# Rows of the main expert slots turned by DMA in 16-bit planes, in place of transposes on TensorE

## The chip, the cores and the metric

The kernel runs on one core of one Trainium2 chip. Its time is the device time of one execution in microseconds (us). Three executions of the kernel before took 737.18 to 739.1 us, with a median of 738.54 us. A fourth execution, taken with the hardware profiler, took 740.14 us; all rows below come from it.

## The reference

The kernel computes feature-map attention and sends the result through a mixture of eight experts, everything in float32. Cut to what matters:

```
q_p, k_p = phi(q), phi(k)                 # exp(+-(x @ w_phi - max|x @ w_phi|))
x  = (q_p @ (k_p^T v)) / (q_p . sum k_p)  # 8 x 8 heads, 576 tokens of 64 -> 4608 tokens of 512
logits = x @ w_gate;  local = sigmoid(x @ w_local)
e  = argmax(logits) if first token or local < 0.5 else the expert of the token before
out = softmax(logits)[e] * (relu(x @ w1[e]) @ w2[e])   # w1[e]: 512 x 1024, w2[e]: 1024 x 512
```

## The kernel before

**Two halves.** The first half (to about 290 us) is the attention and the gate. It writes the 4608 rows of x (512 floats each) to DRAM as `xs`. The second half is the mixture of experts, and only its later part is touched by the change.

**Slots.** Tokens are sorted by expert into units of 128 rows. A slot is one expert with the units that it works on: a quad has 4 units, a trip 3, a pair 2. A dual is one unit of two half-filled experts, and reads both experts' weights. Two early trips run while the gate is being finished. Then the method `moe` runs the eleven main slots, one after another: quad Q0, trip T0, dual D0, Q1, T1, Q2, D1, T2, Q3, T3 and the pair P.

**A slot's work.** `layer1` multiplies the slot's transposed rows with eight column blocks of w1 and `layer2` multiplies the result unit by unit with w2. Every float32 product is made of three products of two-part numbers (`three`, lines 1114 to 1116: high by high, low by high, high by low). So each operand is needed as a high part (rounded by ScalarE) and a low part (the rest, subtracted by VectorE). A quad's layer 1 is 8 x 12 matmuls of 512 columns, a trip's 8 x 12 of 384 columns; layer 2 is 24 matmuls of 512 columns for each unit. The results `y` of a unit are scaled by VectorE (line 1216) and scattered to DRAM by an indirect DMA on GpSimd's queue (`out`, line 1219).

**Weights.** Each slot reads eight blocks of 512 KB on SyncE's queue (line 980) into raw buffers `wraw` (five of them). ScalarE rounds a block (`whi`, line 991) and VectorE subtracts (`wlo`, line 994) into one of thirteen pairs of buffers. Blocks are loaded ahead, as soon as buffers come free. A dual's blocks go straight into the pairs, sixteen DMAs of 512 KB.

**The rows of the next slot.** They are fetched by an indirect DMA on GpSimd's queue (`gather_x`, line 1038) as token by feature tiles `xg`, 128 x 512, of which there are six buffers. TensorE must have them as feature by token. `tokens` does this: it hands `layer2` of the slot in front a list of steps, and after the first three matmuls of layer 2 a step transposes up to four units in TensorE, eight transposes of 64 rows a unit (`rows`, line 1096), into PSUM tiles `tr`. `parts` then makes the high part on ScalarE (line 1109, or 1107 for a dual) and the low part on VectorE (line 1110). Where the next slot is a dual, the dual's unit and those of the slot behind it are prepared together, during the slot in front of the dual. So 28 of the main slots' 32 units are transposed in this way, in eight places: 3 in Q0, 4 + 1 in T0, 3 in Q1, 4 in T1, 4 in Q2, 4 in T2, 3 in Q3 and 2 in T3. Q0's own four units are transposed earlier, by another method.

**Order.** A scheduler places the instructions of each engine; the method `past` holds an instruction behind a marked one on its own engine. Each engine works its instructions off in order, and DMAs issued by one engine stand in that engine's queue.

Of the kernel before, what the change touches and what calls it, by code (L numbers as in the profile page):

```python
# [7 lines left out]
F32 = mybir.dt.float32  # L8
F32R = mybir.dt.float32r
BF16 = mybir.dt.bfloat16  # L10
I32 = mybir.dt.int32
AF = mybir.ActivationFunctionType
ALU = mybir.AluOpType
AX = mybir.AxisListType
# [4 lines left out]
DM, E, FF = 512, 8, 1024  # L19
# [37 lines left out]
class Kernel:  # L57
# [9 lines left out]
    def run(self):  # L67
        nc, tc, A = self.nc, self.tc, self.A
        act, dve = self.act, self.dve
        with ExitStack() as root:  # L70
# [13 lines left out]
            warm = self.const.tile([128, E], BF16, name="warm")  # L84
            act.activation(warm, self.cnt, AF.Exp)

# [182 lines left out]
    def proj(self, p):  # L269
# [18 lines left out]
        for sg in (0, 1):  # L288
            self.last_act = act.activation(kp[:, :, :, sg, :].rearrange("p c h f -> p h c f"), sb[:, :, :, 0], AF.Exp,  # L289
                                           scale=1.0 - 2 * sg)  # L290
# [17 lines left out]
    def qexp(self, p, pj):  # L308
# [3 lines left out]
        for sg in (0, 1):  # L312
            self.act.activation(qp[:, sg].rearrange("p h (c r k) -> p (h c) r k", c=2, r=2), src, AF.Exp,  # L313
                                scale=1.0 - 2 * sg)
# [265 lines left out]
    def gate(self, bp):  # L580
        tc, pe, act, dve, pool, ident = self.tc, self.pe, self.act, self.dve, self.pool, self.ident

        def sm(shape, name, dt=F32):
            return self.small.tile(shape, dt, name="g_" + name)
# [51 lines left out]
        yield  # L636
        ci = sm([9, 128], "ci", I32)
        dve.tensor_scalar_max(ci, sc, cm)
# [32 lines left out]
        yield  # L671
        ri = self.back2.tile([128, NC], I32, name="ri")
        dve.tensor_copy(ri, rf)
# [3 lines left out]
        ex = sm([128, NC, E], "ex")  # L677
        act.activation(ex, ls, AF.Exp)
        yield
# [61 lines left out]
    def experts(self, es, name):  # L741
        ei = self.psm([NU, 1], "ei" + name, I32)
        self.dve.tensor_scalar_min(ei, es, float(E - 1))
        return ei

    def fetch(self, es, k, n, name, wait, halves=()):
# [3 lines left out]
        dve.scalar_tensor_tensor(row, es, float(NU_E), k, ALU.mult, ALU.add)  # L750
        ri = self.psm([NU, 1], "ri" + name, I32)

# [26 lines left out]
        t = self.pst([128, 2, n])  # L779
        tok = self.psm([128, n], "tok" + name, I32)  # L780
        prob = self.psm([128, n], "prob" + name)
# [7 lines left out]
    def units_so_far(self, add, shift, name):  # L789
# [4 lines left out]
        t = self.moved(t, [NU, E], "u" + name)  # L794
        u = self.psm([NU, E], "u" + name, I32)
        with self.soon():
# [272 lines left out]
    def tokens(self, slots, late=False):  # L1069

        for s in slots:
            if "xg" not in s:
                self.gather_x(s)
        units, g = [(s, k) for s in slots for k in range(s["n"])], 1 if late else 4

        def step(group):
            if late:
                self.whole(*group[0], group[0][1] % 3 == 2, self.here())
                return
            out = []  # L1080
            for n, (s, k) in enumerate(group):
                if n % 2 == 0:
                    t = self.halfbanks()
                c = slice(n % 2 * 256, n % 2 * 256 + 256)
                out.append((s, k, t[:, :, c]))
                self.rows(out[-1][2], s["xg"][k])
            for s, k, t in out:
                self.unrow(s, *self.into(s), k * 128, t)
        return [lambda a=a: step(units[a:a + g]) for a in range(0, len(units), g)]

    def rows(self, t, src):

        for d in range(4):
            for r in (0, 1):
                k = slice(64 * r, 64 * r + 64)
                self.pe.transpose(t[:, r, d * 64:d * 64 + 64], src[k, d * 128:d * 128 + 128], self.ident[k, k])  # L1096
# [40 lines left out]
    def layer1(self, s, between):  # L1137
# [9 lines left out]
        for f0 in range(0, 8, per):  # L1147
# [10 lines left out]
            hc = slice(f0, f0 + per)  # L1158
            self.marks[act] = act.activation(hh[:, hc, :], t, AF.Relu)  # L1159
            self.marks[dve] = dve.scalar_tensor_tensor(hl[:, hc, :], t, 0.0, hh[:, hc, :].bitcast(F32),  # L1160
# [5 lines left out]
    def layer1_one(self, s, between):  # L1166
# [7 lines left out]
        def turn(q):  # L1174
            t = self.halfbanks()[:, :, 0:256]
            self.rows(t, hs[:, q * 512:q * 512 + 512])
            hc = slice(q * 4, q * 4 + 4)
            self.unrow(s, hh[:, hc], hl[:, hc], 0, t)
        for q in range(4):
            t = self.psl.tile([128, 256], F32, name="l1")  # L1180
            for d in range(4):
                self.both(s, q, t, xh[:, d, x], xl[:, d, x], slice(d * 256, d * 256 + 256), d == 0, d == 3)
                if d == 0 and q == 3:
                    turn(0)
            self.marks[act] = act.activation(hs[:, q * 256:(q + 1) * 256], t, AF.Relu)
            if between:
# [5 lines left out]
    def layer2(self, s, between, held=None):  # L1192
        tc, dve, pool = self.tc, self.dve, self.pool
        hh, hl = s["h"]
        self.need(s, 8) if len(s["ei"]) == 1 else None
        for k in range(s["n"]):
            if hasattr(self, "psr"):
                t = self.psr.tile([128, DM], F32, name="l2")
            else:
                t = self.psb.tile([128, DM], F32, name="l2", tag="nm")  # L1200
            o = slice(k * 128, k * 128 + 128)
            for f in range(8):
                c = slice((f % 2) * DM, (f % 2) * DM + DM)
                self.both(s, 4 + f // 2, t, hh[:, f, o], hl[:, f, o], c, f == 0, f == 7)
                if f in ((0, 2) if s["n"] > 1 else (1, 3, 5)) and between:
                    between.pop(0)()
                if f % 2 and k == s["n"] - 1:
                    self.used(1)
                elif f % 2:
                    self.spare()  # L1210
            y = self.mx2.tile([128, DM], F32, name="y", bufs=3)
            u = s["u"] + k
            if s in self.eslots:
                self.marks[self.act] = self.act.mul(y, t, s["prob"][:, u:u + 1])
            else:
                self.marks[dve] = dve.tensor_scalar_mul(y, t, s["prob"][:, u:u + 1])  # L1216

            def put(y=y, at=s["tok"][:, u:u + 1]):
                ins = pool.indirect_dma_start(self.A["out"], bass.IndirectOffsetOnAxis(at, 0), y, None,  # L1219
                                              bounds_check=NT - 1, oob_is_err=False)  # L1220
                tc.declare_no_dep(ins.ins, group="outs", reason="each token is written once")
                tc.add_to_no_dep_group("outs", ins.ins)
            if held is None:
                put()
            else:
                held.append(put)

    def slots(self, order, held=None, soon=(), later=()):
        first = order[0]
        if "x" not in first:  # L1230
            if first is self.eslots[0]:
                self.first_tokens(first)
            else:
                for f in self.tokens([first]):
                    f()
        self.held = first.get("asked", len(first.get("w", ())))
        self.coming, self.loaded = list(order), getattr(self, "loaded", [])
        self.marks = {self.sp: self.marks[self.sp]} if soon or held is not None else {}
        for i, s in enumerate(order):
            while s.get("asked", len(s.get("w", ()))) < 8:  # L1240
                self.spare()
            self.need(s, 4)
            new = order[i + 1] if i + 1 < len(order) else None
            ahead = order[i + 1:i + 3 if new and len(new["ei"]) == 2 and s["n"] > 1 else i + 2]
            between = self.tokens([x for x in ahead if "x" not in x], bool(soon) and i == 0)
            if s["n"] > 1:
                self.layer1(s, list(soon[i]) if i < len(soon) else [])
                rest = between
            else:
                rest = self.layer1_one(s, between) + between  # L1250
            if i < len(later):
                rest = list(later[i]) + rest
            self.layer2(s, rest, None if new else held)
            for f in rest:
                f()
            s.clear()
# [131 lines left out]
```

## Time and profile before

| what | value |
|---|---|
| median of three executions | 738.54 us (737.18 to 739.1) |
| profiled execution | 740.14 us, of which the span is 738.4 us |
| granted TensorE clock over the span | 0.998 of full speed |
| TensorE matmul busy | 718.3 us (97%) |
| VectorE, ScalarE, GpSimd busy | 446.8, 348.9, 183.2 us |
| DMA, mean over the span | 169 GB/s |

The span runs from the first to the last instruction of the program; 1.7 us lie around it. A main slot shows in the timeline of TensorE as a run of `l<-xhi,..` matmuls (layer 1) and a run of `l<-whi,hh` matmuls (layer 2). The main slots take the span from 363 us to its end.

### The profile page before, as it was taken

To read this page: it belongs to the slowest core of one execution; us is meant where nothing else is said; L and a number is where in the kernel's file an instruction comes from. 1 tells how busy PE (TensorE), PEld (TensorE's weight loads), DVE (VectorE), ACT (ScalarE), POOL (GpSimd) and SP (SyncE) were. 2 spreads that over 40 slices of the span, in tenths; PEclk is the share of its full clock that TensorE was granted. 3 is DMA by queue.
4 is the path that set the end of the run, shared out by engine and by line. 5 is a ranking of instruction groups with operands and counts; after the bars stand their busy time and mean duration, and the time that the engine had idled before them with its cause. 6 is when DMAs were issued, how large, how long until landed. Compare 5 with 4: busy or idle time off the path is not lost.

```text
span 738.4 us, 22173 instructions
## 1 busy us (share of the span) xinstructions
PE 718.3 (97%) x9447; PEld 630.2 (85%) x9447; DVE 446.8 (61%) x814; ACT 348.9 (47%) x673; POOL 183.2 (25%) x305
## 2 busy tenths in 40 slices
PE   7999999999989999999999999999999999999996
PEld 6999999999979988888888975889888778888995
DVE  5898898889978885583436335445523365444413
ACT  4777776777667763333534125333312245241301
POOL 0211002420265674363403041021302102101011
PEclk9999999999999999999999999999999999999999
DMA  7765544555476842064819966335676365434100
GB/s 208 230 188 143 159 133 136 152 150 143 131 250 189 250 136 66 10 214 133 317 65 335 327 235 221 122 129 172 226 296 242 120 220 171 143 128 158 58 40 30
DMA packets 66101, 125.05 MB, mean 169 GB/s; under 512 B 7220, under 2 KB 45300, under 8 KB 65950
## 3 DMA queue, kind: packets, MB, share of 16 engines
q1 hardware_dynamic: 57808, 101.03, 43.1%
q0 software_dynamic: 8016, 22.51, 8.6%
q8 instruction: 75, 1.23, 0.7%
q14 instruction: 26, 0.21, 0.1%
q10 hardware_dynamic: 176, 0.07, 0.0%
HBM read 102.05 MB, written 22.06 MB: 168 GB/s over the span
## 4 chain that ended last, share of the span: by engine, by line
PE 52%; issue 0%; DVE 0%; POOLq 0%; another core or an unknown queue 0%; POOL 0%
PE l L1114 16%; PE l L1115 15%; PE l L1116 15%; PE l L1127 4%; PE tr L1096 1%; PE tr L1066 0%; DVE wlo L994 0%; POOLq L1384 0%; DVE y L1216 0%; POOLq L1302 0%; POOLq L1303 0%; POOL out L1219 0%; POOLq L1219 0%
## 5 line engine op out<-in xcount | busy, mean ns | idle before, releaser
L1159 ACT ACTIVATE hh<-l 128x384 fp32r<-128x384 f32 (+1 forms) x84 | 45.1, 537 | 197.4 <-PE l L1116 161.2
L1114 PE MATMUL l<-xhi,whi 128*128 128x384 f32 (+2 forms) x352 | 123.8, 352 | 0.0
L1116 PE MATMUL l<-xhi,wlo 128*128 128x384 f32 (+2 forms) x352 | 123.2, 350 | 0.0
L1115 PE MATMUL l<-xlo,whi 128*128 128x384 f32 (+2 forms) x352 | 123.1, 350 | 0.0
L1160 DVE SCALAR_TENSOR_TENSOR hl<-l,hh 128x384 fp32r<-128x384 f32 (+1 forms) x84 | 51.6, 614 | 116.6 <-ACT hh L1159 113.5
L994 DVE TENSOR_TENSOR wlo<-wraw,whi 128x1024 fp32r<-128x1024 f32 x80 | 96.6, 1223 | 32.3 <-ACT whi L991 32.0
L1114 PE MATMUL l<-whi,hh 128*128 128x512 f32 x288 | 114.1, 396 | 0.0
L1115 PE MATMUL l<-wlo,hh 128*128 128x512 f32 x288 | 112.4, 390 | 0.3 <-DVE wlo L994 0.3
L1116 PE MATMUL l<-whi,hl 128*128 128x512 f32 x288 | 112.4, 390 | 0.0
L289 ACT ACTIVATE kp<-sb 128x512 f32<-128x512 f32 x144 | 83.4, 624 | 59.4 <-DVE sb L285 51.9
L283 DVE TENSOR_REDUCE m<-pj 128x8 f32<-128x1024 f32 x72 | 87.9, 1221 | 26.9 <-PE pj L280 22.1
L991 ACT CAST whi<-wraw 128x1024 fp32r<-128x1024 f32 x80 | 82.1, 1047 | 29.3 <-PE l L1116 14.9
L285 DVE TENSOR_TENSOR sb<-pj,m 128x1024 f32<-128x1024 f32 x72 | 88.2, 1225 | 4.4
L408 PE MATMUL nm<-kvs,qp 128*64 128x74 f32 x2304 | 88.7, 228 | 2.1 <-issue 1.5
L280 PE MATMUL pj<-first,kq 64*128 64x128 f32 x1152 | 85.8, 290 | 4.6 <-DMA kq<-in_kqT 4.2
L313 ACT ACTIVATE qp<-pj 128x512 f32<-128x512 f32 x144 | 79.9, 597 | 13.4 <-PE pj L298 12.5
L1219 POOL DMA_INDIRECT out<-y,p_tokm x32 | 36.9, 1154 | 198.8 <-DVE y L1216 179.2
L408 PEld LDWEIGHTS nm<-kvs,qp 128*64 128x64 f32 x2304 | 80.7, 136 | 3.2 <-issue 2.1
L280 PEld LDWEIGHTS pj<-first,kq 64*128 64x128 f32 x1152 | 72.0, 192 | 10.6 <-issue 4.1
L330 PE MATMUL kvp<-v,kp 128*64 128x65 f32 x2048 | 77.3, 226 | 1.5 <-issue 1.3
L1114 PEld LDWEIGHTS l<-xhi,whi 128*128 128x128 f32 x352 | 66.2, 188 | 7.0 <-issue 1.6
L330 PEld LDWEIGHTS kvp<-v,kp 128*64 128x64 f32 x2048 | 67.5, 139 | 4.7 <-issue 1.5
(226 smaller groups left out, 916.5 us busy)
## 6 DMA issues: line engine op xcount, KB each, us to landing
wraw<-in_w1h SPq DMA_DIRECT2D x44, 512.0 KB
wraw<-in_w2h SPq DMA_DIRECT2D x44, 512.0 KB
kq<-in_kqT SPq DMA_DIRECT2D x47, 384.0 KB
v<-in_va SPq DMA_DIRECT2D x48, 195.0 KB
xs<-xo SPq DMA_DIRECT2D x48, 128.0 KB
whi<-in_w1h SPq DMA_DIRECT2D x8, 512.0 KB
wlo<-in_w1h SPq DMA_DIRECT2D x8, 512.0 KB
whi<-in_w2h SPq DMA_DIRECT2D x8, 512.0 KB
```

Source lines behind the costliest of these rows:

```text
L280: self.last_pe = self.pe.matmul(t[:, h, i % 2, j, :], kq[r, j, s], self.w2[r], start=True, stop=True)
L283: dve.tensor_reduce(m, f, AX.X, ALU.max, apply_absolute_value=True)
L285: self.last_dve = dve.tensor_sub(sb.rearrange("p h c j f -> p (h c j) f"), f, m.unsqueeze(2).broadcast_to([128, 8, 128]))
L289: self.last_act = act.activation(kp[:, :, :, sg, :].rearrange("p c h f -> p h c f"), sb[:, :, :, 0], AF.Exp, scale=1.0 - 2 * sg)
L313: self.act.activation(qp[:, sg].rearrange("p h (c r k) -> p (h c) r k", c=2, r=2), src, AF.Exp, scale=1.0 - 2 * sg)
L330: self.pe.matmul(t[r, sg, h], kp[:, h, sg, r], v[:, h], start=first and sg + h == 0, stop=last and sg + h == 2)
L408: self.last_num = self.pe.matmul(e["t"][r, c - c0, k], self.ch[i]["qp"][:, sg, h, q0 + r.start:q0 + r.stop], kvs[:, sg, k], start=sg == 0, ...
L991: self.act.copy(hi, raw)
L994: (low or self.dve).tensor_sub(lo[:, c], raw[:, c], hi.bitcast(F32)[:, c])
L1114: mm(o, ah, bh, start=first, stop=False)
L1115: mm(o, ah, bl, start=False, stop=False)
L1116: self.last_pe = mm(o, al, bh, start=False, stop=last)
```

## The change

`tokens` is kept for the first main slot, for the early slots and for a rare loop behind the main slots. For the 28 units named above, `turned` takes its place:

- GpSimd copies each gathered tile (128 x 512 float32, seen as 1024 16-bit numbers a row) into a tile `xz` in which the 512 low halves come first and the 512 high halves behind them (line 1100).
- SyncE issues a transposing DMA of `xz` back into the gathered tile `xg` (line 1107), behind the weight load that was issued last: eight blocks of 128 x 128 16-bit numbers. It is placed in layer 1 of the slot in front, from its eighth pause on, one at every second pause.
- VectorE copies the turned planes back into float32 order, into another tile `xz` (line 1114). ScalarE and VectorE make the high and low parts from that tile, as before from PSUM. These steps stand where the transposes stood, one unit to a step in place of four.

The planes and the joined tiles share two buffers `xz`. The tile `y` has two buffers in place of three.

```
+            x = self.ml1.tile([128, 2, DM], U16, name="xz", bufs=2)
+            self.pool.tensor_copy(x, s["xg"][k].bitcast(U16).rearrange("p (d z) -> p z d", z=2))
...
+            with self.past(self.sp):
+                self.marks[self.sp] = self.sp.dma_start_transpose(t, planes[i].rearrange("p z d -> p (z d)"))
...
+            x = self.ml1.tile([128, 4, 128, 2], U16, name="xz", bufs=2)
+            with self.past(self.dve):
+                self.dve.tensor_copy(x.rearrange("p d t z -> p z d t"),
+                                     s["xg"][k].bitcast(U16).rearrange("p (z d t) -> p z d t", z=2, t=128))
+            x = x.rearrange("p d t z -> p d (t z)").bitcast(F32)
+            self.parts(s, hi, lo, slice(k * 128, k * 128 + 128), x)
+        no = lambda: None
+        first = [no] * 7
+        for i in range(len(units)):
+            first += [lambda i=i: turn(i), no]
+        return first, [lambda i=i: join(i) for i in range(len(units))]
...
-            y = self.mx2.tile([128, DM], F32, name="y", bufs=3)
+            y = self.mx2.tile([128, DM], F32, name="y")
...
-            between = self.tokens([x for x in ahead if "x" not in x], bool(soon) and i == 0)
+            ahead = [x for x in ahead if "x" not in x]
+            if soon and i == 0:
+                first, between = list(soon[i]), self.tokens(ahead, True)
+            elif i < len(soon):
+                first, between = list(soon[i]), []
+            else:
+                first, between = self.turned(ahead)
             if s["n"] > 1:
-                self.layer1(s, list(soon[i]) if i < len(soon) else [])
+                self.layer1(s, first)
```

On TensorE the 224 transposes of line 1096 with `xg` as input go, and nothing else changes its order. Two places on other engines follow.

SyncE's queue during T1's layer 1 and behind it, before: the last weight loads of Q2 (`in_w2h`), the read of D1's expert numbers, and D1's first load.

```order
L980 DMA wraw_8279<-in_w2h 128x1024
L980 ISA
L980 DMA wraw_8330<-in_w2h 128x1024
L980 ISA
L980 DMA wraw_8366<-in_w2h 128x1024
L980 ISA
L980 DMA wraw_8402<-in_w2h 128x1024
L967 TENSOR_LOAD p_eih0_6606
```

The same place after the change, with four transposing DMAs, one for each unit of Q2:

```order
L981 DMA wraw_8298<-in_w2h 128x1024
L1107 DMA_TRANSPOSE xg_8246<-xz_8254 128x8x128
L981 ISA
L981 DMA wraw_8335<-in_w2h 128x1024
L1107 DMA_TRANSPOSE xg_8248<-xz_8256 128x8x128
L1107 DMA_TRANSPOSE xg_8250<-xz_8258 128x8x128
L981 ISA
L981 DMA wraw_8373<-in_w2h 128x1024
L1107 DMA_TRANSPOSE xg_8252<-xz_8260 128x8x128
L968 TENSOR_LOAD p_eih0_6606
```

The first transposing DMA stands behind the second of the four loads, the next two behind the third, the last behind the fourth and in front of everything that D1 reads.

VectorE at the end of T1's layer 1 and in its layer 2, before: `hl` is the low part of layer 1's result, `wlo` of a weight block, `xlo` of a unit of Q2, and `y` a unit's result.

```order
L1160 SCALAR_TENSOR_TENSOR hl_8295<-l1_8419,hh_8294 128x384
L994 TENSOR_TENSOR wlo_8435<-wraw_8279,whi_8434 128x1024
L1110 TENSOR_TENSOR xlo_8499<-tr_8464,xhi_8498 128x4x128
L1110 TENSOR_TENSOR xlo_8499<-tr_8481,xhi_8498 128x4x128
L1110 TENSOR_TENSOR xlo_8499<-tr_8464,xhi_8498 128x4x128
L1110 TENSOR_TENSOR xlo_8499<-tr_8481,xhi_8498 128x4x128
L994 TENSOR_TENSOR wlo_8512<-wraw_8330,whi_8511 128x1024
L1216 TENSOR_SCALAR y_8533<-l2_8460,p_probm_6836 128x512
L1216 TENSOR_SCALAR y_8563<-l2_8538,p_probm_6836 128x512
```

The same place after the change:

```order
L1193 SCALAR_TENSOR_TENSOR hl_8263<-l1_8391,hh_8262 128x384
L1114 COPY xz_8438<-xg_8246 128x2x512
L995 TENSOR_TENSOR wlo_8407<-wraw_8239,whi_8406 128x1024
L1143 TENSOR_TENSOR xlo_8437<-xz_8438,xhi_8436 128x4x128
L995 TENSOR_TENSOR wlo_8446<-wraw_8298,whi_8445 128x1024
L1114 COPY xz_8452<-xg_8248 128x2x512
L1249 TENSOR_SCALAR y_8471<-l2_8432,p_probm_6836 128x512
L1143 TENSOR_TENSOR xlo_8437<-xz_8452,xhi_8436 128x4x128
L1114 COPY xz_8480<-xg_8250 128x2x512
L1143 TENSOR_TENSOR xlo_8437<-xz_8480,xhi_8436 128x4x128
L1114 COPY xz_8490<-xg_8252 128x2x512
L1249 TENSOR_SCALAR y_8509<-l2_8476,p_probm_6836 128x512
```

Four copies (line 1114) are new, each waiting for a turned tile; two of them stand in front of the first `y`, and two in front of the second.

## Rows read from the trace of the kernel before

**Rows 1.** Page: its head, and TensorE's busy time, share and instructions.

```profile
span 738.4 us, 22173 instructions
PE 718.3 (97%) x9447; PEld 630.2 (85%) x9447; DVE 446.8 (61%) x814; ACT 348.9 (47%) x673; POOL 183.2 (25%) x305
```

**Rows 2.** Windows: stretch, us; PE, PEld, DVE, ACT, POOL busy; clock; DMA share; GB/s.

```profile
364.00:710.00 346.00, 346.00 (x1886) 285.46 (x1885) 153.49 (x183) 115.89 (x168) 56.54 (x52) 1.00 0.53 187
...
400.00:420.00 20.00, 20.00 (x106) 18.67 (x105) 6.74 (x9) 4.57 (x7) 2.46 (x3) 1.00 0.99 362
```

**Rows 3.** Timeline of TensorE at the transposes of Q0 and T0: start, us, instructions.

```profile
384.84 0.39 PE L1114 MATMUL l<-whi,hh 128*128 128x512 f32 x1
...
385.29 0.39 PE L1116 MATMUL l<-whi,hl 128*128 128x512 f32 x1
385.61 0.96 PE L1096 MATMUL tr<-first,xg 64*128 64x64 f32 x24
...
386.84 0.40 PE L1115 MATMUL l<-wlo,hh 128*128 128x512 f32 x1
...
424.84 0.40 PE L1116 MATMUL l<-whi,hl 128*128 128x512 f32 x1
425.17 1.20 PE L1096 MATMUL tr<-first,xg 64*128 64x64 f32 x32
...
426.64 0.39 PE L1115 MATMUL l<-wlo,hh 128*128 128x512 f32 x1
...
427.56 0.40 PE L1116 MATMUL l<-whi,hl 128*128 128x512 f32 x1
427.89 0.46 PE L1096 MATMUL tr<-first,xg 64*128 64x64 f32 x8
...
428.62 0.39 PE L1115 MATMUL l<-wlo,hh 128*128 128x512 f32 x1
```

**Rows 4.** Groups of instructions: shapes, count | busy us, mean ns | idle before.

```profile
L994 DVE TENSOR_TENSOR wlo<-wraw,whi 128x1024 fp32r<-128x1024 f32 x80 | 96.6, 1223 | 32.3 <-ACT whi L991 32.0
L1110 DVE TENSOR_TENSOR xlo<-tr,xhi 128x512 fp32r<-128x512 f32 x36 | 24.1, 686 | 7.6 <-issue 3.0 <-ACT xhi L1107 2.5 <-ACT xhi L1109 2.0
L493 POOL TENSOR_TENSOR wlo<-wraw,whi 128x256 fp32r<-128x256 f32 x32 | 22.7, 729 | 7.6 <-ACT whi L491 7.0 <-ACT p_toke L570 0.5
```

**Rows 5.** DMA queues from 364 to 710 us: packets, MB, share of 16 engines.

```profile
DMA packets 18277, 64.74 MB, mean 187 GB/s; under 512 B 2525, under 2 KB 2525, under 8 KB 18253
q1 hardware_dynamic: 13933, 50.72, 42.1%
q0 software_dynamic: 4320, 13.71, 10.7%
```

**Rows 6.** DMA queues from 291 to 294 us, where short rows are stored.

```profile
q1 hardware_dynamic: 672, 0.33, 37.1%
```

**Rows 7.** Waits of SyncE's queue from 364 to 710 us: us, times, longest.

```profile
SPq L980 <- DVE wlo L994: 205.4, 28, 17.3
```

**Rows 8.** Timeline: the tightest split, in Q0; a split for Q1, its first use.

```profile
385.67 0.69 DVE L1160 SCALAR_TENSOR_TENSOR hl<-l,hh 128x512 fp32r<-128x512 f32 x1 [2.03 <-ACT hh L1159]
386.60 1.22 DVE L994 TENSOR_TENSOR wlo<-wraw,whi 128x1024 fp32r<-128x1024 f32 x1 [0.24 <-ACT whi L991]
...
438.12 1.22 DVE L994 TENSOR_TENSOR wlo<-wraw,whi 128x1024 fp32r<-128x1024 f32 x1
...
457.80 0.50 PE L1114 MATMUL l<-xhi,whi 128*128 128x512 f32 x1
```

**Rows 9.** Timeline of SyncE's queue and of TensorE around T1's layer 2.

```profile
501.52 13.18 SPq L980 DMA_DIRECT2D wraw<-in_w2h  x4
516.10 0.33 SPq L980 DMA_DIRECT2D whi<-in_w1h  x1
...
519.25 0.39 PE L1114 MATMUL l<-whi,hh 128*128 128x512 f32 x1
...
536.96 0.39 PE L1114 MATMUL l<-xhi,whi 128*128 128x512 f32 x1
```

More of the change, by code (lines that the diff above doesn't have):

```diff
@@ L11 @@
 I32 = mybir.dt.int32
+U16 = mybir.dt.uint16
 AF = mybir.ActivationFunctionType
@@ L1089, in tokens, with turned, turn, join @@
         return [lambda a=a: step(units[a:a + g]) for a in range(0, len(units), g)]
+    def turned(self, slots):
+        for s in slots:
+            self.gather_x(s)
+        units = [(s, k) for s in slots for k in range(s["n"])]
+        planes = []
+        for s, k in units:
+            x = self.ml1.tile([128, 2, DM], U16, name="xz", bufs=2)
+            self.pool.tensor_copy(x, s["xg"][k].bitcast(U16).rearrange("p (d z) -> p z d", z=2))
+            planes.append(x)
+        def turn(i):
+            s, k = units[i]
+            t = s["xg"][k].bitcast(U16).rearrange("p (j t) -> p j t", t=128)
+            with self.past(self.sp):
+                self.marks[self.sp] = self.sp.dma_start_transpose(t, planes[i].rearrange("p z d -> p (z d)"))
+        def join(i):
+            s, k = units[i]
+            hi, lo = self.into(s)
+            x = self.ml1.tile([128, 4, 128, 2], U16, name="xz", bufs=2)
[9 more added lines that the diff above has]
+        return first, [lambda i=i: join(i) for i in range(len(units))]
     def rows(self, t, src):
```

## The prediction

> **What bounds the kernel now.** I read the page's busy times first: the reader is to see TensorE busy 97% of the span and no other engine above 61% [rows 1]. That is a mean over two halves, so the next view is the busy time of the stretch that the change touches, 364 to 710 us: TensorE is busy in all 346 of 346 us at the full clock, VectorE in 153, ScalarE in 116, GpSimd in 57, the DMA engines at 53% [rows 2]. A modelled busy time can hide gaps, so the timeline of TensorE comes next: the matmuls of 512 columns follow each other every 0.225 us (384.84 to 385.29, two steps) with nothing between them but the transposes [rows 3]. TensorE is the bound, and every instruction taken from it shortens the stretch, as long as what takes its place arrives in time. What could arrive late is read from the queue of weights, from VectorE's order and from the DMA share.
>
> **What goes.** The 224 transposes stand in eight places. Their cost is not their busy time, since they overlap; it is what they push the next matmuls back. In Q0 24 transposes lie between matmuls at 385.29 and 386.84, 1.55 us for two steps that otherwise take 0.45: 1.10 us. In T0 32 of them cost 426.64 - 424.84 - 0.45 = 1.35 us, and 8 of them 428.62 - 427.56 - 0.45 = 0.61 us [rows 3]. Places with 24 are Q0, Q1, Q3; with 32 T0, T1, Q2, T2; with 8 T0 a second time; with 16 T3, put at 0.86 us between 0.61 and 1.35. The sum is 3 x 1.10 + 4 x 1.35 + 0.61 + 0.86 = 10.2 us. All of it is on the path, because TensorE waits for nothing there. The rest of TensorE's order is as it was.
>
> **What is added, and what covers it.**
>
> GpSimd: 28 copies of 1024 16-bit numbers a row. The nearest row is its subtraction of 256 float32 in 0.73 us [rows 4]. By bytes a copy would take 1.46 us, by elements 2.9 us, and with a single input perhaps as little as 0.7. I take 1.5 us, the value by bytes; 28 of them are 42 us, 81 at the upper end, on an engine that has 289 us free [rows 2]. Cost 0.
>
> VectorE: 28 copies of 1024 numbers. The nearest row by elements is 1.22 us (a weight split), by bytes 0.69 us (a low part) [rows 4]. I take 1.22: 34 us, where 192 are free [rows 2]. It reads the low parts from SBUF in place of PSUM; no gain is counted. The place to look at is the tightest split: in Q0 one of 1.22 us begins at 386.60, and VectorE was free from 386.36 [rows 8]. It serves the fourth pair of layer 2, whose use comes some 19 matmuls after 384.84, at about 389.1 without the transposes. A copy of 1.22 us in front of it ends at 387.6, the split at 388.8: just in time, late by up to 0.5 us if the copy is slower. The splits for T0 to T3 are ready 14 us or more ahead of their use; one for Q1 stands for them, ready at 439.34 and used at 457.80 [rows 8].
>
> The weights' queue: 28 transposing DMAs of 256 KB. No row shows one. At the rate of the present loads (50.72 MB in 42.1% of 346 us, 348 GB/s) one takes 0.75 us [rows 5]. Its pieces are short, 1024 of 256 bytes. Stored rows of 512 bytes took 37.1% of 16 engines' 3 us for 672 packets, 26.5 ns each [rows 6]; at that price for a shorter piece a transpose takes 1024 x 26.5 / 16 = 1.7 us. At the price of a long packet (42.1% x 16 x 346 us / 13933 = 167 ns [rows 5]) it would be 10.7 us. I take 1.7 us, from the row with the nearest size: 48 us in all. The queues use 42.1 + 10.7% of the stretch, so 163 us are free [rows 5], or 5.8 us a transpose.
>
> Behind a transposing DMA stand weight loads, and it makes them wait: for GpSimd's copy, and in the queue itself. Loads already wait for buffers most of the time, 205 us for splits alone [rows 7], and the split for Q1 has 18 us in hand. A delay of 3 to 6 us in a slot does not reach TensorE. The narrowest stretch is 400 to 420 us, where D0's sixteen blocks take 99% of the DMA engines at 362 GB/s [rows 2]; the transposes that fall there are those of D0 and Q1, used 20 us and more later.
>
> The chain that must be in time is longest in T1, with four units and a short layer 2. Only two planes fit the two buffers, so the third and fourth copies of GpSimd wait until the first and second transposes have landed. The second transpose stands behind the third load, at about 514 us (the four loads end at 514.7 [rows 9]). With D from issue to landing and 2.9 us for the copy, the fourth lands by 514 + 2D + 2.9. Two joins of some 2.5 us each (copy 1.22, low part 0.69 [rows 4], a rounding on ScalarE) end at 522 + 2D. Q2's layer 1 begins at 536.96 [rows 9], 1.35 us sooner without T1's transposes: D may be 6.8 us. With 1.7 us in the queue, 5 us are left for everything else.
>
> The result tile with two buffers: a unit's 24 matmuls take 5.4 us, so a scatter has about 10 us until its buffer is written again. GpSimd's scatter takes its turn behind copies that wait for joins, but those are over within that time. Cost 0, up to 1 us in a slot if a join is late.
>
> **Sum.** The profiled execution took 740.14 us: 740.14 - 10.2 = 729.9. The median of the runs lies 1.6 us lower, at 738.54, so 728.3; with 0.7 us for the tight split and a late join here and there (bounds 0 and 3), 729.0 us.
>
> [...] The rows give 32 transposes, that is four units, 1.35 us on TensorE [rows 3]. [...]
>
> **Rivals.**
>
> *The transposes are slow and the weights' queue becomes the bound.* For it: nothing in this trace shows such a DMA, its upper end is 10.7 us, and weights and transposes share one queue that works in order. Against it: the 512-byte rows cost 26.5 ns. The point from which it decides is 5.8 us a transpose, when the 163 free us are used up; from 6.2 us on the kernel is slower than before. At 8 us, the queue is short by 28 x 8 - 163 = 61 us: 738.5 - 10.2 + 61 = 789 us; at 10.7 us by 137: 865 us. Just past D = 6.8 us the late start of Q2 and its like (two slots with four units in a trip's layer 2) costs a few us each: about 740.
>
> *TensorE's 10.2 us come back as waits.* In T1 two of VectorE's copies stand in front of the first `y`. If each of the eight layers 2 lost 1.3 us, because the copy waits for a landing and holds the weight split or `y` behind it, the time would be 738.5 - 10.2 + 10.4 = 739. For it: VectorE works in order, and the second copy waits for the last transpose. Against it: that `y` is not due before 519.25 + 5.4 us [rows 9], and its bank is not wanted until 5.4 us later.
>
> *The change doesn't take its time off the path* can hardly be: the transposes are gone from TensorE's order, and nothing in 364 to 710 us runs beside them that TensorE waits for.
>
> **How the numbers follow.** Forecast, with all of the new work hidden: 0.66, own range 726.5 to 732. Part of the gain lost to waits, but still faster by over 0.3% (under 736.3; about what a measurement can tell from no change): 0.05. Waits that eat the gain: 0.08. Slow transposes: 0.21. So faster 0.71, same 0.08, slower 0.21. The range reaches to 741, just past the mild end of the slow case, and leaves its long end out.
>
> **What would show it.** Right: no transposes of `xg` on TensorE between 385 and 710 us, the layers 2 of T1 and Q2 shorter by 1.4 us each, TensorE without waits for `xhi`, `xlo` or `wlo`, and transposing DMAs that raise the DMA share by some 14 points (48 of 346 us). Wrong: SyncE's queue in which weight loads follow a transposing DMA many us later; TensorE waiting at the head of Q2, Q3 or T2 for `xlo`; `wlo` splits that wait for the landing of weights. A transposing DMA over 6 us would overturn the forecast by itself.

## The result, and the profile after

| | before | after |
|---|---|---|
| median of 5 runs, us | 738.9 (737.18 to 740.26) | 728.98 (728.19 to 730.17) |
| the profiled execution, us | 740.14 | 730.11 |
| its span, us | 738.4 | 728.3 |

The ratio of after to before is 0.9872, with a 95% interval of 0.9857 to 0.9888: the kernel is 1.3% faster, 9.9 us by the medians. 729.0 was forecast, with faster as the likeliest case.

The head of the page after answers to [rows 1], the stretch rows to [rows 2]. The stretch begins at 364 us as before and ends at 700, since layer 2 of T3 ends 10 us earlier.

```profile
span 728.3 us, 21882 instructions
PE 707.5 (97%) x9223; PEld 623.2 (86%) x9223; DVE 471.2 (65%) x842; ACT 350.6 (48%) x673; POOL 224.9 (31%) x333
```

Busy time in two stretches of after, columns as in [rows 2]:

```profile
364.00:700.00 336.00, 336.00 (x1664) 278.81 (x1663) 176.22 (x210) 117.56 (x168) 96.07 (x78) 1.00 0.71 214
400.00:420.00 20.00, 20.00 (x108) 18.83 (x107) 7.33 (x11) 4.96 (x8) 4.32 (x3) 1.00 1.03 385
```

TensorE is busy in 336 of 336 us, as in 346 of 346 before, at the full clock in both, and has 224 instructions less (9447 - 9223). GpSimd and VectorE have more to do, and the DMA share rises from 53 to 71%. TensorE's timeline at the same two places as [rows 3], first Q0, then T0:

```profile
384.96 0.39 PE L1147 MATMUL l<-whi,hh 128*128 128x512 f32 x1
385.19 0.39 PE L1148 MATMUL l<-wlo,hh 128*128 128x512 f32 x1
385.42 0.39 PE L1149 MATMUL l<-whi,hl 128*128 128x512 f32 x1
385.64 0.39 PE L1147 MATMUL l<-whi,hh 128*128 128x512 f32 x1
...
425.01 0.40 PE L1148 MATMUL l<-wlo,hh 128*128 128x512 f32 x1
425.24 0.39 PE L1149 MATMUL l<-whi,hl 128*128 128x512 f32 x1
425.47 0.39 PE L1147 MATMUL l<-whi,hh 128*128 128x512 f32 x1
```

The steps of 0.225 us now go on where the transposes stood. From the first matmul of each layer 2 to that of the next slot, read from the two timelines:

| layer 2 of | Q0 | T0 | Q1 | T1 | Q2 | T2 | Q3 | T3 | sum |
|---|---|---|---|---|---|---|---|---|---|
| before, us | 22.87 | 18.41 | 22.89 | 17.71 | 23.23 | 17.72 | 22.89 | 17.20 | |
| after, us | 21.76 | 16.45 | 21.76 | 16.36 | 21.85 | 16.36 | 21.76 | 16.36 | |
| less by | 1.11 | 1.96 | 1.13 | 1.35 | 1.38 | 1.36 | 1.13 | 0.84 | 10.26 |
| forecast | 1.10 | 1.96 | 1.10 | 1.35 | 1.35 | 1.35 | 1.10 | 0.86 | 10.17 |

All layers 1 from Q0 on agree within 0.03 us. Outside these there are two differences. The slot ahead of Q0 is 0.88 us longer (19.75 for 18.87 us), because TensorE waits there once. This is the only wait of TensorE from 300 us on (us in total, times, longest); its one wait for the same operation before was 0.3 us:

```profile
PE l L1148 <- DVE wlo L995: 1.2, 1, 1.2
```

And the first matmul of the first expert slot came at 289.83 in place of 290.58 us, 0.75 us earlier, in a part that the change doesn't touch; in the executions profiled below that moment lies anywhere from 283.7 to 286.5 us, so it is put down to chance. -10.26 + 0.88 - 0.75 makes -10.13; the profiled executions differ by 10.03 us.

What was added, by groups from 364 to 700 us, answering to [rows 4] (two of GpSimd's copies lie before it):

```profile
L995 DVE TENSOR_TENSOR wlo<-wraw,whi 128x1024 fp32r<-128x1024 f32 x63 | 78.9, 1267 | 20.7 <-ACT whi L992 20.4 <-issue 0.3
L1100 POOL COPY xz<-xg 128x1024 uint16<-128x1024 uint16 x26 | 28.7, 1105 | 73.7 <-DMA xg<-xz 71.5 <-DVE xlo L1143 1.6 <-POOL xz L1100 0.7
L1114 DVE COPY xz<-xg 128x1024 uint16<-128x1024 uint16 x28 | 21.1, 756 | 1.4 <-DMA xg<-xz 1.2
L1143 DVE TENSOR_TENSOR xlo<-xz,xhi 128x512 fp32r<-128x512 f32 x26 | 20.6, 795 | 7.9 <-ACT xhi L1142 6.3 <-issue 1.4
```

The queues of that stretch, answering to [rows 5], and the short pieces of one transposing DMA with nothing beside it in its queue (T1's fourth), from 517.8 to 519 us:

```profile
DMA packets 47761, 71.76 MB, mean 214 GB/s; under 512 B 32087, under 2 KB 32087, under 8 KB 47736
q1 hardware_dynamic: 43424, 57.77, 58.9%
q0 software_dynamic: 4312, 13.67, 11.9%
...
DMA packets 912, 0.24 MB, mean 201 GB/s; under 512 B 911, under 2 KB 911, under 8 KB 911
q1 hardware_dynamic: 911, 0.23, 83.8%
```

Alone, a short piece takes 0.838 x 16 x 1.2 us / 911 = 17.7 ns, so 1024 of them 1.1 us of 16 engines. Among the loads they cost (0.589 x 336 - 0.421 x 346) / 28 = 1.9 us each. SyncE's queue around T1, answering to [rows 9], and its waits, answering to [rows 7]:

```profile
498.48 2.21 SPq L1107 DMA_TRANSPOSE xg<-xz  x1
509.77 0.36 SPq L981 DMA_DIRECT2D wraw<-in_w2h  x1
510.24 3.70 SPq L1107 DMA_TRANSPOSE xg<-xz  x2
514.14 0.42 SPq L981 DMA_DIRECT2D wraw<-in_w2h  x1
516.40 1.24 SPq L1107 DMA_TRANSPOSE xg<-xz  x1
519.37 0.34 SPq L981 DMA_DIRECT2D whi<-in_w1h  x1
...
SPq L981 <- DVE wlo L995: 164.1, 26, 14.0
```

A load leaves the queue in 0.33 us; a transposing DMA holds it for 1.23 us at least. The 28 hold it for 47.5 us, 1.7 each. The queue had that time to spare here: its waits for splits fall from 205 to 164 us, and TensorE feels none of it.

### The profile page after: what moved, and what is told of

Read it like the earlier page. It is cut to its first block, busy times and chain, and to the rows that moved or that the text cites. A ratio compares the mean times of both kernels' runs of the same rounds, so it can differ in the third digit from the quotient of the medians.

```text
span 728.3 us, 21882 instructions
## 1 busy us (share of the span) xinstructions
PE 707.5 (97%) x9223; PEld 623.2 (86%) x9223; DVE 471.2 (65%) x842; ACT 350.6 (48%) x673; POOL 224.9 (31%) x333
## 4 chain that ended last, share of the span: by engine, by line
PE 51%; DVE 0%; issue 0%; POOLq 0%; another core or an unknown queue 0%; POOL 0%
PE l L1148 16%; PE l L1147 16%; PE l L1149 15%; PE l L1160 4%; DVE wlo L995 0%; PE tr L1067 0%; PE tr L1129 0%; POOLq L1423 0%; DVE y L1249 0%; POOLq L1341 0%; POOL out L1252 0%; POOLq L1342 0%; POOLq L1252 0%
## 5 line engine op out<-in xcount | busy, mean ns | idle before, releaser
L995 DVE TENSOR_TENSOR wlo<-wraw,whi 128x1024 fp32r<-128x1024 f32 x80 | 100.1, 1268 | 26.0 <-ACT whi L992 25.7
L1252 POOL DMA_INDIRECT out<-y,p_tokm x32 | 42.4, 1325 | 138.7 <-DVE y L1249 119.8
```

Of the source, the lines that this page charges most:

```text
L995: (low or self.dve).tensor_sub(lo[:, c], raw[:, c], hi.bitcast(F32)[:, c])
```

## The experiments

In the runs of all experiments the kernel before took 734.2 to 734.3 us, 4 to 5 us less than above. Only ratios to it are compared; the changed kernel has 0.9877 there (0.9854 to 0.9899, f3_after).

**Is it TensorE's time?** e1_dead puts the transposes back, of a constant (one step for up to four units, as before):

```
+ for n in range(len(units[i:i + 4])): ... self.pe.transpose(t[...], self.ident[k, :], self.ident[k, k])
  join(i)
```

> The changed kernel with 224 transposes of a constant put back on TensorE at the eight places where the kernel before had its own; nobody reads them, and the new path by GpSimd, the transposing DMAs and VectorE stays. Theory (the gain is TensorE's time for the transposes, all of it on the path): the stages grow back by 10.2 us, 728.98 + 10.2 = 739.2 us. Rival (the gain comes from elsewhere, as from VectorE and ScalarE reading the tokens from SBUF rather than from PSUM, or from waits that the transposes made): it stays near 729, at most 732 us.

Measured: 1.0018 (1.0004 to 1.0032). The theory holds, the rival falls: the new path alone gives nothing. The eight layers 2 take 23.42, 18.41, 22.91, 17.70, 23.25, 17.73, 22.87 and 17.19 us, the old lengths but for Q0's, which is 0.55 longer than before. TensorE waits there 0.2 us for `y`; it waits 0.3 us for `wlo` in the slot ahead.

**Does the smaller `y` cost?** e7_y2 is the kernel before with that alone:

```
- y = self.mx2.tile([128, DM], F32, name="y", bufs=3)
+ y = self.mx2.tile([128, DM], F32, name="y")
```

> The kernel before with two buffers for the result tile y in place of three, which is the part of the change that makes room for the planes; nothing else. Theory: no cost, 738.9 us within 0.5. Rival (the two buffers cost part of what the transposes give back): 740 us or more, with VectorE waiting before y for the store of two units earlier.

Measured: 0.9998 (0.9985 to 1.0011). No cost, as the theory had it, to within 1 us.

**How much room has the queue?** e2_x2 and e3_x4 put more transposing DMAs behind each of the 28 (range(3), range(8)):

```
+ for _ in range(3):
+     x = self.ml1.tile([128, 3, 128], U16, name="xd", bufs=2)
+     self.marks[self.sp] = self.sp.dma_start_transpose(x, planes[i]...[:, 0:384])
```

> The changed kernel with three more transposing DMAs of 384 columns behind each of the 28, into two tiles that nobody reads: 2.1 times the columns. Theory (the queue has room: 98 us of the 16 engines are free from 364 to 700 us, and 28 x 1.1 x 1.9 = 59 us are added): the same within 1 us, 729 to 730 us. Rival (a transposing DMA costs the weights' queue so much that it is nearly the bound, by landings that each next piece waits for and by issues of more than a microsecond): weights arrive late and TensorE waits for wlo and whi, 735 us or more.

> The changed kernel with eight more transposing DMAs of 384 columns behind each of the 28: 4 times the columns. Theory (5.8 us of queue for a unit is the point from which it decides): 28 x 3 x 1.9 = 160 us are added where 98 are free, so the queue is short by some 60 us and TensorE waits for weights: 770 to 830 us. Rival (transposes run beside the weight loads without taking from them): 729 to 732 us.

Measured: 1.0305 (1.0273 to 1.0336) and 1.2324 (1.229 to 1.2359). e3_x4 is over the edge as expected, by more than expected (905 us for 770 to 830). e2_x2 went against the theory: 31 us are lost, with the weights' DMA queue at a share of only 67.3%. Two suspects were left, the queue's time and the extra reads, which keep the planes' two buffers from the joins. f1_free1 and f2_free3 read a constant in place of the planes, one and three extra:

```
+     self.marks[self.sp] = self.sp.dma_start_transpose(x, self.settled.bitcast(U16)[:, 0:384])
```

> The changed kernel with one more transposing DMA of 384 columns behind each of the 28. Unlike in e2_x2 it reads a constant, so it holds no plane, and its two tiles are read by nobody. Theory (what e2_x2 lost, it lost for two reasons: issuing one holds SyncE's queue for 1.25 us whatever its columns, and its extra reads kept the planes' two buffers from the joins; SyncE's queue waits for splits during 164 of 336 us, so 28 x 1.25 = 35 us in single pieces find room): at most 3 us over the changed kernel, a ratio to the kernel before of 0.987 to 0.991. Rival (the queue has no room at all): 28 x 1.25 us come through in good part, a ratio of 1.01 or more.

> As f1_free1 with three more behind each of the 28, so the same count and columns as e2_x2, without its hold on the planes. Theory (both reasons count): the fourth unit of a T slot is turned some 12 us later than in the changed kernel where 6 are in hand, so TensorE waits for xhi at D0, Q2 and Q3, but less than in e2_x2: a ratio of 1.00 to 1.02. Rival 1 (the queue is all of it): as e2_x2, 1.03. Rival 2 (the held planes are all of it): as the changed kernel, 0.987.

Measured: 0.9867 (0.9841 to 0.9892) with one, as the theory had it, and 1.0288 (1.025 to 1.0325) with three, against it. With three the held planes are ruled out as the main cause, and so is the theory that both count alike: e2_x2 and f2_free3 agree within their intervals. What the traces show in place of it is SyncE's queue. The extra DMAs load the 16 engines, too (the weights' queue takes 69.3% of them from 364 to 700 us in f2_free3, 58.9% in the changed kernel), and no run adds that load without the queue's time, so a part of the engines in the 30 us isn't excluded. The extra tiles and the queue's waits in f2_free3 (first row: ns min/median/max of one):

```profile
L1112 SPq DMA_TRANSPOSE xd<-first x84: 1177/1234/1982, 361.4 to 708.2; - x84
...
SPq L982 <- DVE wlo L996: 61.3, 18, 12.1
SPq L1112 <- DMA xd<-first: 41.5, 21, 4.5
```

384 columns hold the queue as long as 1024 do: 1234 ns by the median, 1284 in the changed kernel. Per unit the queue is held for 1.7 us in the changed kernel, 3.1 in f1_free1, 5.5 in f2_free3 (the time of all transposing DMAs over 28), there with 1.5 us more of waiting for the extra tiles (41.5 / 28). At 3.1 one slot shows it, D0, whose layer 1 takes 8.50 for 7.50 us. In f2_free3 that layer takes 21.26 us. Its SyncE and ScalarE rows in f2_free3, and the wait within it, with TensorE's granted clock around its end, 0.50 (last row, columns as in [rows 2]):

```profile
439.06 6.67 SPq L1112 DMA_TRANSPOSE xd<-first  x3
446.75 2.29 SPq L982 DMA_DIRECT2D wraw<-in_w1h  x4
...
443.27 1.24 ACT L1147 CAST xhi<-xz 128x512 fp32r<-128x512 f32 x2 [2.26 <-DVE xz L1119]
451.05 1.04 ACT L993 CAST whi<-wraw 128x1024 fp32r<-128x1024 f32 x1 [6.54 <-DMA wraw<-in_w1h]
452.00 0.38 ACT L1223 ACTIVATE hs<-l 128x256 f32<-128x256 f32 x1
...
452.43 0.69 PE L1165 MATMUL l<-whi,xhi 128*64 128x256 f32 x1 [11.28 <-ACT hs L1223]
...
450.00:455.00 5.00, 2.57 (x12) 1.48 (x14) 1.52 (x2) 2.70 (x5) 0.00 (x0) 0.50 0.93 338
```

The reader is to see a chain through three engines that work in order: the loads for Q1 leave SyncE's queue only at 446.75 us, behind T0's five units; ScalarE stands before the split of the first until 451.05; behind that split stands D0's `hs`, which the split has nothing to do with; and TensorE waits 11.28 us for `hs`. Counted from T0's first matmul, these loads leave after 44.3 us here, after 23.7 in the changed kernel (430.45 - 406.72) and after 14.3 before the change (421.98 - 407.71). From the first of T0's transposing DMAs to these loads 39.0 us pass here, and for 28.6 of them the twenty transposing DMAs hold the queue.

The wait costs more than itself. From 450 to 455 us, in the last 2.4 us of it and the first 2.6 behind it, TensorE's granted clock is 0.50 (last row), and until 456.3 us a step takes 0.43 us in place of the 0.21 ahead of the wait: so D0 loses 13.8 us by a wait of 11.3. Q2's layer 2 loses another 8.9 us; there `y` stands behind copies that wait 8.7 and 4.1 us for their landings, and steps behind are slow again (0.43 us for 0.23, 580.94 to 583.07 and 590.34 to 593.33). The other places lose 0.7 to 2.2 us each and were not followed up. The runs that lose time by long waits all have a lower clock over the span: 0.982 to 0.988 in the profiled executions of e2_x2, f2_free3, e6_late and e8_actq, 0.909 in e3_x4, and 0.997 in the changed kernel.

**Whose queue, and when?** e8_actq issues the 28 from ScalarE; e6_late issues them in layer 2:

```
- self.marks[self.sp] = self.sp.dma_start_transpose(...)      # e8_actq
+ self.marks[self.act] = self.act.dma_start_transpose(...)
...
- first += [lambda i=i: turn(i), no]                          # e6_late: first is empty
+ return [], turns[:2] + [x for p in zip(joins, turns[2:]) for x in p] + joins[-2:] ...
```

> The changed kernel with the transposing DMAs issued from ScalarE's queue in place of SyncE's. Theory (issuing one holds a queue for 1.24 us and for the wait on the planes; SyncE's queue has that time, ScalarE's order does not, since hh stands behind it and layer 1 has two banks): ScalarE stands still for up to some 4 us at the third and fourth unit, and TensorE waits for hh: 733 to 742 us. Rival (any queue will do, and the weight loads are even earlier): 728 to 729 us.

> The changed kernel with the transposing DMAs of a slot issued in its layer 2 in place of its layer 1, joins between them. Theory (what hides the transposes is that they start a layer early; the way from issue over landing, copy, low part takes some 6 us a pair and the steps of a T slot's layer 2 are 16 us): for the slots with four units behind a T slot (Q2, Q3) the last two joins come 2 to 4 us late, TensorE waits there for xhi or xlo, elsewhere not: 733 to 737 us. Rival (the place doesn't matter, since the DMA is short): 729 to 730 us. A third way: the transposes stand behind weight loads that wait for splits, and all slots are late: 745 us or more.

Measured: 1.0182 (1.015 to 1.0213) from ScalarE, 1.0249 (1.0219 to 1.0279) in layer 2, both slower than before the change. For e8_actq the direction was right and the price too small (some 22 us over the changed kernel by the ratios, 4 to 13 expected). ScalarE's order in T0's layer 1:

```profile
413.84 3.85 ACTq L1107 DMA_TRANSPOSE xg<-xz  x1
417.74 0.49 ACT L1192 ACTIVATE hh<-l 128x384 fp32r<-128x384 f32 x1 [3.54 <-issue]
422.92 1.25 ACTq L1107 DMA_TRANSPOSE xg<-xz  x1
424.21 0.49 ACT L1192 ACTIVATE hh<-l 128x384 fp32r<-128x384 f32 x1 [5.98 <-issue]
...
443.02 0.80 PE L1147 MATMUL l<-whi,hh 128*128 128x512 f32 x1 [8.15 <-DVE y L1249]
```

`hh` stands behind the issue and what the issue waits for, layer 1 drags on, and so the copies, landings and joins are late as well: VectorE waits 9.91 us for a landing, `y` stands behind it, and TensorE waits 8.15 us for the bank that `y` is to clear. For e6_late the theory's 733 to 737 us were too low; the third way was nearest, though not all slots are late. In T1 the first transposing DMA leaves 14.6 us after the slot's first matmul (519.90, 505.3), behind weight loads that wait for splits; in the changed kernel it leaves with that matmul (498.48, 498.51):

```profile
505.53 11.95 SPq L981 DMA_DIRECT2D wraw<-in_w2h  x4
...
519.90 6.35 SPq L1107 DMA_TRANSPOSE xg<-xz  x2
...
528.66 3.74 SPq L1107 DMA_TRANSPOSE xg<-xz  x2
...
543.92 0.79 PE L1145 MATMUL l<-xhi,whi 128*128 128x512 f32 x1 [5.41 <-ACT xhi L1140]
```

TensorE waits for `xhi` at the heads of T0, Q2 and Q3 (3.1, 5.4 and 8.0 us) and loses time at D0, too; the heads of the other slots are not late.

**Where does the new wait come from?** In the slot ahead of Q0, GpSimd's first two copies and three weight splits meet. VectorE's rows after, then GpSimd's; before the change the three took 3.50 us. In this trace only the second copy lies under a split, the first, which takes 2.05 us for 1.22:

```profile
345.67 4.32 DVE L995 TENSOR_TENSOR wlo<-wraw,whi 128x1024 fp32r<-128x1024 f32 x3 [0.39 <-ACT whi L992]
...
344.36 1.04 POOL L1100 COPY xz<-xg 128x1024 uint16<-128x1024 uint16 x1 [1.47 <-PE l L1149]
345.60 1.04 POOL L1100 COPY xz<-xg 128x1024 uint16<-128x1024 uint16 x1 [0.20 <-DMA xg<-xs,p_tokm]
```

e4_planes gives the kernel before (with two buffers for `y`) the 28 GpSimd copies and nothing else; e5_defer and f4_defer, one kernel, put the first three of the changed kernel behind GpSimd's last store:

```
+ x = self.ml1.tile([128, 2, DM], mybir.dt.uint16, name="xz", bufs=2)        # e4_planes
+ self.pool.tensor_copy(x, s["xg"][k].bitcast(mybir.dt.uint16).rearrange("p (d z) -> p z d", z=2))
+ with self.tc.issue_after(self.lastput.ins) if "t0" not in self.__dict__ else nullcontext():   # e5, f4
      self.pool.tensor_copy(x, ...)
```

> The kernel before with two buffers for y and with the 28 GpSimd copies that part the rows into planes; nobody reads the planes, and the tokens are turned on TensorE as before. Theory (a copy of GpSimd stops VectorE's operations that read two tiles in SBUF, and only the one place at 346 us, where three weight splits in a row are urgent, hands it on to TensorE): the wait for wlo at 348 us grows from 0.3 to some 1.2 us, the other collisions are hidden: 738.9 + 0.9 = 739.8 us. Rival (that wait came from the transposing DMAs or from chance): the wait stays 0.3 us, 738.9 us.

> The changed kernel with the first three plane copies on GpSimd put behind its last store of the slot before, some 16 us later; they are not needed before 400 us. Theory (they collide with the three urgent splits): splits of 4.32 us shrink to 3.5, TensorE's wait for wlo at 348 us from 1.2 to 0.3 us: 728.98 - 0.9 = 728.1 us. Rival (the wait has another cause): the wait stays 1.2 us, 729.0 us.

> The changed kernel once more, as the base for the others on the same chip: a ratio of 0.987, in the trace a wait of TensorE for wlo of 0.7 to 1.2 us at the slot before Q0 and none after it.

> e5_defer once more, beside the changed kernel on the same chip. Theory (the collision of GpSimd's first copies with three weight splits costs TensorE 0.9 us): no wait for wlo, 0.7 to 0.9 us below the changed kernel, which is near what the runs can tell. Rival: no difference, with the same wait in the trace.

Measured: e4_planes 1.0006 (0.9993 to 1.0019), e5_defer 0.9867 (0.9843 to 0.9892), f3_after 0.9877 (0.9854 to 0.9899), f4_defer 0.9871 (0.9849 to 0.9892). The times don't tell these apart; the medians of f3_after and f4_defer, side by side, are 724.69 and 724.71 us. The traces do. The splits in f3_after, then in f4_defer:

```profile
338.96 4.84 DVE L995 TENSOR_TENSOR wlo<-wraw,whi 128x1024 fp32r<-128x1024 f32 x3 [0.38 <-ACT whi L992]
```

```profile
339.67 3.50 DVE L995 TENSOR_TENSOR wlo<-wraw,whi 128x1024 fp32r<-128x1024 f32 x3 [0.38 <-ACT whi L992]
```

The layer 2 ahead of Q0 then takes 18.39 us where f3_after has 19.46, and TensorE has no wait from 300 us on. (In f3_after it has two of 0.3 us; one of 0.7 to 1.2 was expected.) In the kernel before, the copies alone lengthen that layer 2 from 18.37 (e7_y2) to 19.20 us. So the collision is shown, and its 0.8 to 1.1 us in that slot. The 0.7 to 0.9 us that f4_defer was to be faster are not: what the runs can tell is coarser, and the start of the first expert slot alone varies by over 2 us between the profiled executions.

## Why the prediction was right, point by point

*What goes* was right in size and place: 10.26 us measured for 10.17, place by place, and e1_dead brings it back.

*GpSimd's copies* take 1.04 us, not 1.5. "Cost 0" missed one thing: a copy isn't only GpSimd's time. Beside one, a weight split of VectorE, which reads two tiles in SBUF, took 2.05 us for 1.22. That cost TensorE 0.88 us, 18 us before the stretch that was looked at: the free GpSimd took its first copies long before Q0, under three splits that were urgent.

*VectorE's copies* take 0.75 us, not 1.22, below the upper end and near the lower. The tight split in Q0 was in time: a copy from 386.40 to 387.15, splits to 388.25, and Q0's layer 2 has its plain length. So the 0.7 us for a late split was spent, but in another slot and for another reason; that the sum came out at 729.0 is in part luck of this kind, and so are the 0.75 us by which the first half happened to be shorter in the profiled pair. One join waited for a landing, 1.2 us, and TensorE didn't feel it.

*The transposing DMA* was taken at 1.7 us of the engines: 1.1 alone and 1.9 among the loads. The row of 512-byte stores [rows 6] was the right neighbour, and the price by long packets, 10.7 us, was far off.

*The weights' queue* was priced in the wrong coin. "5.8 us a transpose" divided the DMA engines' free time evenly over the stretch. In that coin a unit of f2_free3 costs some (0.667 x 360 - 0.421 x 346) / 28 = 3.4 us (364 to 724 us, where its T3 ends), well below 5.8, and 30 us are lost all the same. What ran short is SyncE's time, which the sum had no term for, and first in one narrow place, T0's five units ahead of Q1's loads; 3.1 us of it a unit show there (f1_free1, 1.0 us in D0), 5.5 with the waits and the lower clock behind them cost 30 us. The first rival was thus nearer than 5.8 us made it; the delay of Q1's loads by some 9.5 us, counted from T0's first matmul (23.7 for 14.3), is more than the 3 to 6 foreseen, and still hidden by the 18 us in hand [rows 8].

*The chain in T1* held: the second transposing DMA left at 510.24 us, 11.7 us after T1's first matmul at 498.51, where the forecast's 514 us lies 11.4 after it (502.58 before). The fourth left at 516.40, its join began at 524.17, and Q2 began at 531.54. Issue to join was 7.8 us, but most of that is VectorE's and ScalarE's order; the data had landed by about 519.

*Rival 2*, gain lost in waits, needed a landing later than this one: f2_free3 and e8_actq show its way (`y` behind a copy that waits), the changed kernel doesn't. *Rival 3* falls with e1_dead. *`y` with two buffers* costs nothing, as said (e7_y2).

*What would show it*: the DMA share of the engines rose by 18 points (53 to 71%), where 14 were forecast; the rest came as described, but for the one wait for `wlo` ahead of Q0.

## What to carry to other kernels

Where one engine is busy without a gap, work taken from it is worth what it pushed back, place by place, and here the trace of before gave that within 0.1 us. What is added has to be priced in the coin of each thing that works in order: how long the issuing queue is held, whose instructions stand behind it, and which narrow slot comes next; a free share over the stretch says little. And a copy on an idle GpSimd was not free for VectorE here (up to 1.19 us on a split of 1.22): look for what both do at the same moment, also ahead of the place that was changed. Where TensorE must wait long, count slower steps behind the wait as well (in f2_free3 0.43 us for 0.21, behind 11.3 us).

## What the runs showed of the hardware

Issuing a transposing DMA held the queue for 1.2 to 1.3 us, of 384 columns in f2_free3 as of 1024 in the changed kernel (1177 to 1234 ns and 1232 to 1284 ns, least and median), where a plain load of the changed kernel held it for 0.33 (median).

TensorE stood still in f2_free3 from 441.15 to 452.43 us. Its granted clock was 0.50 from 450 to 455 us, with matmuls running again for the second half of that. The same matmuls of 256 columns followed each other every 0.21 us before (437.75 to 440.77), every 0.43 us from 452.91 to 456.32, and every 0.21 us again from 457.66.

Where GpSimd copied 16-bit numbers from SBUF to SBUF beside a split or a low part of VectorE, which read two tiles in SBUF, that operation took longer at eleven places of the changed kernel, by the time that both ran to within some 0.15 us. Two of them lie behind T1, VectorE first, then GpSimd:

```profile
525.60 1.11 DVE L1143 TENSOR_TENSOR xlo<-xz,xhi 128x512 fp32r<-128x512 f32 x1 [0.69 <-ACT xhi L1142]
526.63 0.74 DVE L1249 TENSOR_SCALAR y<-l,p_probm 128x512 f32<-128x512 f32 x1
527.29 2.41 DVE L995 TENSOR_TENSOR wlo<-wraw,whi 128x1024 fp32r<-128x1024 f32 x1
...
525.09 1.06 POOL L1100 COPY xz<-xg 128x1024 uint16<-128x1024 uint16 x1
527.57 1.05 POOL L1100 COPY xz<-xg 128x1024 uint16<-128x1024 uint16 x1
```

A split of 1.22 us takes 2.41 with a copy of 1.05 in its midst, a low part of 0.69 takes 1.11 where 0.55 of it lie under a copy. `y`, which reads a bank of PSUM, keeps its 0.74 us even where it lies wholly under a copy, at 398.66. After 300 us six splits were stretched in this way, by 0.17 to 1.19 us, and five low parts, by 0.41 to 1.08. It goes both ways: a GpSimd copy from 397.67, beneath a split that had begun at 397.53, took 1.96 us for 1.04, while the split kept its 1.21. Which of the two is stretched can't be told from the recorded starts alone: the split at 527.29 began 0.28 us ahead of the copy, too, and there it was the split that took longer.
